# A list scheduler with another model of the engines, and one matmul of a gated unit on 128 rows instead of 64

## The chip, the core and the metric

The program runs on one core of one Trainium2 chip. TensorE (PE) multiplies matrices into PSUM, VectorE (DVE) and ScalarE (ACT) work on tiles, GpSimd (POOL) works on tiles and issues a few DMAs, SyncE (SP) issues the other DMAs. Every engine takes its instructions in the order in which the program lists them for it, and waits where an instruction needs something that isn't ready. The metric is the device time of one execution in microseconds, lower is better.

## The reference

```python
g = sigmoid((u * gate_w).sum(-1))                       # one gate per token
# a: state space convolution, 448 channels, 256 modes each, 2048 tokens
dt = exp(log_dt); A = -exp(log_A_real) + 1j * A_imag; C = (C_real + 1j * C_imag) * dt
K = 2 * einsum("dn,dnl->dl", C, exp(A * dt * pos)).real
a = irfft(rfft(u, 4096) * rfft(K, 4096))[:2048] + u * D_skip
# b: gated linear unit, 448 -> 1792 -> 448
b = (sigmoid(x @ w_gate) * (x @ w_up)) @ w_down
out = g * a + (1 - g) * b
```

All is float32; the outputs have 2048 tokens of 448 channels.

## The kernel before

The kernel has three bodies of work that it runs side by side. An instruction isn't issued where it stands in the source: the source records it by `op` (line 156), with its engine, an estimated duration, what it reads and writes and a priority. `Plan.order` (line 185) then builds the order of all engines by a list schedule: it keeps a clock for each engine, takes the engine that can start something earliest, and on it the ready instruction with the least priority number. `Plan.emit` (line 270) issues them in that order.

**The gated unit** has 14 tiles of 128 hidden units, two halves of 1024 tokens (H), and two blocks of 512 tokens in each (B). Values are split into a high and a low part, each of which TensorE takes in one pass (type float32r); a product is high × high + high × low + low × high. `glu_w` (line 957) loads the weights of a tile, ScalarE rounds them to the high part (`wh`, `vh`, L969), and GpSimd, or VectorE for the last tiles, makes the low part (`wl`, `vl`, L971). `glu_mm` (line 990) multiplies a block of 512 tokens by the weights of 128 hidden units in eleven matmuls. The 448 channels make three blocks of 128 (L995 high × high, L996 high × low, L997 low × high) and one of 64. The last block of the tokens, `x[:, 3]`, holds the high part on the rows 0 to 63 and the low part on the rows 64 to 127, and the weights of these channels stand on both halves of the rows, so L999 does two products at once, and L1000, the eleventh, does low × high. A gate and an up product make one unit (`glu_up`): tanh on ScalarE (L983), the product on VectorE (L984), the split of the result (L986, L987). `glu_down` (line 1005) multiplies back to 448 channels (L1012 to L1014), and VectorE adds the result to `ob` (L1028). There are 112 runs of `glu_mm` and 224 triples of the way down.

**The convolution's kernels.** `params` (line 581) makes the phases and powers of the modes at the start, mostly on VectorE with W = 1024 columns, some on ScalarE and GpSimd. `kgen` (line 895) makes 16 channels at a time, 28 chunks in two halves, each chunk in two half-chunks: phases on TensorE (`tp`, L827, L842), sine and cosine on ScalarE, powers on GpSimd (`tb`, L803 to L816), products of powers and phases on VectorE (L866 to L885), and 32 small matmuls with 32 weight columns each (`kp`, L890). A half's kernels go to DRAM (`kd`).

**The transforms.** A class `Chain` (line 371) takes 224 channels through a two-stage Fourier transform: a first stage with weights on 64 rows (`stage1_pair`, L442, or `stage1_split`, L432 and L433), a transpose (by a detour through DRAM, `shf`, or on VectorE, L453, for the last half), and a second stage with 64 weight columns (`spectrum_pair`, L471). The tokens go first (`spectrum_u`), then each half of the kernels: product with the tokens' spectrum (`product_pair`, L500 to L511) and the way back (`back`, L546, L550). The half 0 works in `fx_fu`, `uax` and `ubx`, the half 1 in `fx_fk`, `ua` and `ub`.

What sets the order is the estimates. TensorE's are c_mm = 0.4167 ns per column and 3 ns, whatever the shape; the 16 small matmuls of a half-chunk are 680 ns; VectorE and GpSimd don't disturb each other; a DMA takes 640 ns to issue and then its bytes at 350 per ns on one wire, with no limit to how many are under way. A change of TensorE's shape, which is the number of rows and of weight columns that a matmul uses (128 × 128, 64 × 128, 128 × 64, 128 × 32), costs nothing in this model. The priorities of the parts are at line 300: parameters 10, kernel generation 20, tokens' transform 30, kernels' transform 40 and 41, gated unit 60, which fills in.

Of the kernel before, what the change touches and what calls it, by code (L numbers as in the profile page):

```python
# [25 lines left out]
SPC, KPC, ACC = 640.0, 680.0, 93.0  # L26
# [12 lines left out]
LN2 = math.log(2.0)  # L39
# [4 lines left out]
# channel order of the kernel generation: (half, chunk, column tile, q)  # L44
# [8 lines left out]
def shape_tables():  # L53
    """Transform matrices and position grids: functions of the shapes alone."""
# [22 lines left out]
        # rows (c g k2) to rows (g c l2), the inverse  # L77
# [17 lines left out]
# functions that one table set of ScalarE holds  # L95
# [3 lines left out]
class Res:  # L99
    """Something that instructions read and write: a virtual tile or a DRAM tensor."""  # L100

    def __init__(self, pool=None, tag=None, shape=None, dt=None, name=None, real=None):
        self.pool, self.tag, self.shape, self.dt, self.name = pool, tag, shape, dt, name
        self.real = real
        self.log = []
        self.users = 0
        self.done = 0.0
        self.live = real is not None
# [8 lines left out]
class Pool:  # L117
    def __init__(self, plan, name, space, after, below):
        self.plan, self.name, self.space, self.after, self.below = plan, name, space, after, below
        self.stack, self.tp = ExitStack(), None  # L120
        self.left, self.end, self.tags = 0, 0.0, {}

    def tile(self, tag, bufs, shape, dt=F32):
        q = self.tags.setdefault(tag, dict(free=[0.0] * bufs, n=0, next=0, bufs=bufs))
# [18 lines left out]

class Plan:
# [11 lines left out]
    def op(self, eng, cost, fn, r=(), w=(), prio=0, after=(), size=0, table=None):  # L156
        me = dict(i=len(self.ops), eng=eng, cost=cost, fn=fn, prio=prio, size=size, table=table,
                  deps=set(), outs=[], res=[], new=[], ready=0.0, order=[a["i"] for a in after])
# [14 lines left out]
        for res in me["res"]:  # L173
            if res.pool is not None:
                res.users += 1
                res.pool.left += 1
# [8 lines left out]
    def order(self):  # L185
        ops = self.ops
        need = []
        for o in ops:
            o["deps"].discard(o["i"])
            o["deps"] |= set(o["order"])  # L190
            for d in o["deps"]:
                ops[d]["outs"].append(o["i"])
            need.append(len(o["deps"]))
        engines = sorted({o["eng"] for o in ops})
        free = {e: 0.0 for e in engines}
        cand = {e: [] for e in engines}
        for o in ops:
            if need[o["i"]] == 0:
                cand[o["eng"]].append(o)
        wire, table, seq, left = 0.0, (), [], len(ops)  # L200

        def start_of(o):
            t = o["ready"]
            for x in o["new"]:
                p = x.pool
                for a in p.after:
                    if a.left:
                        return None
                    t = max(t, a.end)
                q = p.tags[x.tag]  # L210
                if q["next"] != x.idx or not q["free"]:
                    return None
                t = max(t, min(q["free"]))
            return t

        while left:
            best = None
            for e in engines:
# [8 lines left out]
                te = max(lo, free[e])  # L227
# [12 lines left out]
            fin = te + cost  # L240
            if o["size"]:
                wire = max(wire, fin) + o["size"] / 350.0
                fin = wire + 1500.0
            for x in o["new"]:
                q = x.pool.tags[x.tag]
# [894 lines left out]
```

## Time and profile before

| what | value |
|---|---|
| median of 3 runs | 884.44 us (884.14 to 885.29) |
| span of the profiled execution | 878.0 us |
| median less span | 6.4 us |
| mean granted clock of TensorE | 0.972 |
| ScalarE, GpSimd busy | 501.3, 330.1 us |
| DMA | 115.66 MB, 132 GB/s on average |

The profile gives the span from the first instruction to the last of one execution; no other time of that execution is given. A line "L995 PE MATMUL gu_gps<-xs_glu,wh_glu" is the matmul at line 995 that writes the PSUM tile gu of the pool gps from the tiles xs and wh. A matmul's row in the timeline begins at its start; its duration reaches to the modelled end of its last column, while the next one has already started.

### The profile page before, as it was taken

The page shows a single profiled execution, that of the slowest core. Times are in us where ns is not written, and L with a number is a line of the kernel's source. Part 1 is how long each engine was busy: PE and PEld are TensorE (multiplying, and loading weights), DVE is VectorE, ACT ScalarE, POOL GpSimd, SP SyncE. Part 2 cuts the span into 40 slices and gives each one's busy share as a digit, 9 for nine tenths or more (in the row PEclk, how much of TensorE's full clock was granted, in tenths as well). Part 3 has the DMA queues.
Part 4 walks back from the last instruction along what each step waited for, and adds up shares of the span by engine and source line. Part 5 has one row for each costly group of instructions (what it writes and reads, how often), then busy time and mean ns, then how long its engine had stood idle before and what let it go on. Part 6 is the DMA issues. An engine that isn't in the chain of part 4 may idle for free. (4 is left out here: it accounts for less than half of the span.)

```text
span 878.0 us, 16776 instructions
## 1 busy us (share of the span) xinstructions
PE 808.5 (92%) x6688; PEld 541.5 (62%) x6688; DVE 733.0 (83%) x982; ACT 501.3 (57%) x862; POOL 330.1 (38%) x358
## 2 busy tenths in 40 slices
PE   4988799999988999999998999999989999889987
PEld 2665576666655667776665666666766566445543
DVE  2869984798995999999897989899846788978995
ACT  3544654677766877777677987777722352221210
POOL 3367644454452645374355535645021120000000
PEclk9989999899997999999999999999999999998999
DMA  9951377222290326436494116422959953294324
GB/s 242 226 107 32 97 216 168 95 95 93 81 194 26 125 83 146 160 116 157 135 219 120 44 60 180 125 84 79 208 104 248 280 153 109 70 212 119 85 56 117
DMA packets 95831, 115.66 MB, mean 132 GB/s; under 512 B 31465, under 2 KB 80937, under 8 KB 95241
## 3 DMA queue, kind: packets, MB, share of 16 engines
q1 hardware_dynamic: 93704, 110.98, 48.4%
q0 software_dynamic: 2048, 3.61, 1.6%
q8 instruction: 53, 0.87, 0.4%
q14 instruction: 26, 0.20, 0.1%
HBM read 78.32 MB, written 36.24 MB: 130 GB/s over the span
## 5 line engine op out<-in xcount | busy, mean ns | idle before, releaser
L995 PE MATMUL gu_gps<-xs_glu,wh_glu 128*128 128x512 f32 x336 | 148.0, 440 | 11.7 <-ACT wh_glu L969 11.6
L866 DVE TENSOR_TENSOR es_eg<-tb_eg 128x512 f32<-128x512 f32 x168 | 125.5, 772 | 20.7 <-PE kp_egp L890 19.2
L997 PE MATMUL gu_gps<-xs_glu,wl_glu 128*128 128x512 f32 x336 | 135.3, 403 | 1.2 <-POOL wl_glu L971 1.2
L996 PE MATMUL gu_gps<-xs_glu,wh_glu 128*128 128x512 f32 x336 | 135.5, 403 | 0.0
L1012 PE MATMUL dn_gps<-vh_glu,hh_glu 128*128 128x448 f32 x224 | 98.6, 440 | 7.0 <-ACT ob_glu L1021 3.5
L971 POOL TENSOR_TENSOR wl_glu<-xr_glu,wh_glu 128x512 fp32r<-128x512 f32 x44 | 77.8, 1777 | 65.7 <-ACT wh_glu L969 65.7
L995 PEld LDWEIGHTS gu_gps<-xs_glu,wh_glu 128*128 128x128 f32 x336 | 65.6, 195 | 41.2 <-issue 19.0
L1013 PE MATMUL dn_gps<-vh_glu,hl_glu 128*128 128x448 f32 x224 | 83.7, 374 | 4.5 <-DVE hl_glu L987 4.5
L1014 PE MATMUL dn_gps<-vl_glu,hh_glu 128*128 128x448 f32 x224 | 83.6, 373 | 0.5 <-POOL vl_glu L971 0.5
L884 DVE TENSOR_TENSOR ec_eg<-ec_eg,es_eg 128x1024 f32<-128x1024 f32 x56 | 79.8, 1426 | 0.0
L997 PEld LDWEIGHTS gu_gps<-xs_glu,wl_glu 128*128 128x128 f32 x336 | 65.3, 194 | 18.0 <-POOL wl_glu L971 2.8
L813 POOL TENSOR_TENSOR tb_eg<-tb_eg 128x96 f32<-128x96 f32 (+2 forms) x84 | 73.4, 877 | 5.8
L827 PE MATMUL tp_egp<-pos_sb,ph_eg 96*128 96x512 f32 x168 | 72.5, 446 | 1.9 <-ACT fr_eg L845 1.7
L885 DVE TENSOR_TENSOR es_eg<-fr_eg,es_eg 128x1024 f32<-128x1024 f32 x56 | 73.3, 1310 | 0.3
L996 PEld LDWEIGHTS gu_gps<-xs_glu,wh_glu 128*128 128x128 f32 x336 | 65.8, 196 | 10.0 <-issue 1.3
L971 POOL TENSOR_TENSOR vl_glu<-vr_glu,vh_glu 128x448 fp32r<-128x448 f32 x24 | 35.5, 1477 | 87.0 <-ACT vh_glu L969 85.5
L1012 PEld LDWEIGHTS dn_gps<-vh_glu,hh_glu 128*128 128x128 f32 x224 | 42.9, 191 | 39.0 <-issue 17.1
L803 POOL MEMSET tb_eg<- 128x96 f32 x28 | 7.8, 283 | 152.0 <-DVE es_eg L866 152.0
L1028 DVE SCALAR_TENSOR_TENSOR ob_glu<-dn_gps,og,ob_glu 128x448 f32<-128x448 f32 x72 | 49.1, 681 | 18.4 <-PE dn_gps L1014 17.7
L859 ACT ACTIVATE ec_eg<-ec_eg,half_pi 128x1024 f32<-128x1024 f32 x56 | 63.9, 1140 | 0.0
L471 PE MATMUL fps_fups<-fx_fu,m_sb 128*64 128x224 f32 x384 | 48.7, 376 | 15.6 <-DMA fx_fu<-shf 7.8
L984 DVE SCALAR_TENSOR_TENSOR sg_glu<-sg_glu,gu_gps 128x512 f32<-128x512 f32 x56 | 38.1, 682 | 24.8 <-PE gu_gps L1000 18.1
(167 smaller groups left out, 1720.0 us busy)
## 6 DMA issues: line engine op xcount, KB each, us to landing
shf<-fx_fu SPq DMA_DIRECT2D x16, 896.0 KB
fx_fu<-shf SPq DMA_DIRECT2D x16, 896.0 KB
xr_glu<-in_w_dram SPq DMA_DIRECT2D x52, 256.0 KB
us<-fx_fu SPq DMA_DIRECT2D x4, 1792.0 KB
vr_glu<-in_w_dram SPq DMA_DIRECT2D x28, 224.0 KB
gt_pro<-in_u_dram SPq DMA_DIRECT2D x8, 448.0 KB
fx_fu<-in_u_dram SPq DMA_DIRECT2D x8, 448.0 KB
kd<-ke_eg SPq DMA_DIRECT2D x8, 448.0 KB
```

The lines of the kernel that those rows point to most:

```text
L813: pool(96 * m, lambda n=n, m=m: G.tensor_mul(g3(n + 1, m), g3(1, m), g3(n, 1).to_broadcast([128, 32, 3, m])))
L827: T.matmul(tp.real, ph[:, c % 2, 128 * nh:128 * nh + 128].bitcast(F32R), pos[:, 512 * i:512 * i + 512], start=True, stop=last)
L866: V.tensor_mul(o.rearrange("p d (i k) -> p d i k", k=ny), x.unsqueeze(3).to_broadcast([128, 16, nx, ny]), y.unsqueeze(2).to_broadcast([128 ...
L884: op("DVE", c_dve(1024), lambda: V.tensor_mul(ec[:, :, 0:64], ec[:, :, 0:64], es[:, :, 0:64]), [es], [ec], prio)
L885: op("DVE", c_dve(1024), lambda: V.tensor_mul(es[:, :, 0:64], fr.real, es[:, :, 0:64]), [fr], [es], prio)
L971: op(eng, cost(n), lambda: e.tensor_sub(view(l), a(), view(h).bitcast(F32)), [res, (h, key)], [(l, key)], prio)
L995: T.matmul(p.real, wh[:, k, cs], x[:, k], start=(k == 0), stop=False)
L996: T.matmul(p.real, wh[:, k, cs], x[:, 4 + k], start=False, stop=False)
L997: T.matmul(p.real, wl[:, k, cs], x[:, k], start=False, stop=False)
L1012: T.matmul(p[:, :D], hh[:, ts], vh.real, start=(i == 0), stop=False)
L1013: T.matmul(p[:, :D], hl[:, ts], vh.real, start=False, stop=False)
L1014: T.matmul(p[:, :D], hh[:, ts], vl.real, start=False, stop=(i == len(fs) - 1))
```

## The change

Eight things change in the scheduler, all in the estimates and in the rule:

- TensorE: 0.4167 ns per column and 13 ns, float32 matmuls as four passes; a change of shape costs 92, 104 or 196 ns by its neighbours; after a window of 3.4 us with over 1.4 us idle the next one runs at half rate.
- VectorE and GpSimd: instructions with two operands in SBUF hold one port, one engine at a time; fixed times and the times of half-height tiles are set apart.
- SP: 400 ns to issue, at most eight DMAs under way, a rate for each kind of DMA.
- ScalarE: other fixed times for operands in PSUM and for scale or bias by column.
- Delays between engines are 33 to 78 ns and a tail for each engine instead of 200 to 260.
- Buffers of a tile are taken in turn.
- Ten priorities are set apart by a table `RANK`, whose key is engine, tile and old priority.
- The scheduler's state is kept out of the recorded instructions, and most comments are gone.

In the computation one line changes: L1000 multiplies all 128 rows, so that the low part of the weights also meets the low part of the last 64 channels. That adds a product of two low parts, and it writes the same PSUM tile.

```diff
+RANK = {
+    ('Act', 'hh', 45): 41.5,
...
+class Clock:
+    ISSUE, CAST, FLIGHT = 400.0, 600.0, 8
+    WINDOW, IDLE = 3413.0, 1400.0
+    TAIL = dict(PE=175.0, DVE=78.0, Pool=40.0, Act=110.0)
...
+            for hold, port, lead in o["cost"]:
+                t += lead
+                if port:
+                    t = self.port = max(t, self.port) + hold
...
+    def matmul(self, mode, cost, t):
+        if self.mode not in (None, mode):
+            cost += 196.0 if self.fresh else 92.0
+            self.fresh = True
+        elif self.fresh:
+            cost += 104.0
+            self.fresh = False
...
-    HOP, HPE = 200.0, 260.0
+    HOP, HPE, HPOOL = 33.0, 60.0, 78.0
...
-            cost = o["cost"]
-            if o["table"] is not None and o["table"] not in table:
-                table = next(x for x in TABLES if o["table"] in x)
-                cost += 1300.0
-            free[e] = te + cost
...
+            fin = clock.run(o, te)
...
-def c_mm(n, passes=1):
-    return (max(0.4167 * n, 106.0) + 3.0) * passes
+def c_mm(n, count=1, mode=FULL):
+    return [(mode, 0.4167 * n + 13.0)] * count
+def c_mm4(n, count=1, mode=FULL):
+    return [(mode, (1.6667 * n + 4.0) * count * mode[1] / 128)]
...
                 T.matmul(p.real, wh[:, 3, cs], x[:, 3], start=False, stop=False)
-                T.matmul(p.real, wl[0:64, 3, cs], x[0:64, 3], start=False, stop=True)
+                T.matmul(p.real, wl[:, 3, cs], x[:, 3], start=False, stop=True)
```

Every engine's queue is in another order. The counts of the instructions are the same on every engine. Lines of the changed kernel stand 90 further down in these parts: L1000 is L1090 there, L827 is L917, L1012 is L1102, L866 is L956, L318 (every DMA of SP) is L408.

TensorE, where the kernel generation begins (gu: products up, dn: products down, tp: phases). Before:

```order
L999 MATMUL gu_gps_961<-xs_glu_107,wh_glu_869 128x512
L1000 MATMUL gu_gps_961<-xs_glu_107,wl_glu_879 128x512
L1012 MATMUL dn_gps_1004<-vh_glu_628,hh_glu_881 128x448
L1013 MATMUL dn_gps_1004<-vh_glu_628,hl_glu_897 128x448
L1014 MATMUL dn_gps_1004<-vl_glu_633,hh_glu_881 128x448
L995 MATMUL gu_gps_991<-xs_glu_107,wh_glu_869 128x512
L996 MATMUL gu_gps_991<-xs_glu_107,wh_glu_869 128x512
L997 MATMUL gu_gps_991<-xs_glu_107,wl_glu_879 128x512
L827 MATMUL tp_egp_1048<-pos_sb,ph_eg_1002 128x512
L827 MATMUL tp_egp_1052<-pos_sb,ph_eg_1002 128x512
```

After:

```order
L1102 MATMUL dn_gps_1315<-vh_glu_1061,hh_glu_1214 128x448
L1103 MATMUL dn_gps_1315<-vh_glu_1061,hl_glu_1219 128x448
L1104 MATMUL dn_gps_1315<-vl_glu_1068,hh_glu_1214 128x448
L1085 MATMUL gu_gps_1300<-xs_glu_116,wh_glu_1110 128x512
L1086 MATMUL gu_gps_1300<-xs_glu_116,wh_glu_1110 128x512
L1087 MATMUL gu_gps_1300<-xs_glu_116,wl_glu_1119 128x512
L532 MATMUL fps_fups_1340<-fx_fu_1286,ft_fu_1289 128x224 x2
L917 MATMUL tp_egp_1350<-pos_sb,ph_eg_1268 128x512
L917 MATMUL tp_egp_1356<-pos_sb,ph_eg_1268 128x512
L1089 MATMUL gu_gps_1300<-xs_glu_116,wh_glu_1110 128x512
L1090 MATMUL gu_gps_1300<-xs_glu_116,wl_glu_1119 128x512
```

Ahead of the first tp stand 281 products up and 120 down before, and 383 and 192 after, and a first pair of the tokens' transform (L532, on 64 rows) has come ahead of it too.

VectorE at the same place (ob: sums of the gated unit, th and bsx: parameters, es and tb: first chunk). Before:

```order
L593 SCALAR_TENSOR_TENSOR th_pro_917<-th_pro_917,tg_pro_912 128x896
L1028 SCALAR_TENSOR_TENSOR ob_glu_524<-dn_gps_930,og,ob_glu_524 128x448
L747 TENSOR_TENSOR bsx_pro_965<-th_pro_917,ex_pro_899 128x2x14x32
L984 SCALAR_TENSOR_TENSOR sg_glu_958<-sg_glu_958,gu_gps_954 128x512
L1028 SCALAR_TENSOR_TENSOR ob_glu_557<-dn_gps_970,og,ob_glu_557 128x448
```

After:

```order
L1118 SCALAR_TENSOR_TENSOR ob_glu_540<-dn_gps_1247,og,ob_glu_540 128x448
L1074 SCALAR_TENSOR_TENSOR sg_glu_1240<-sg_glu_1240,gu_gps_1235 128x512
L1118 SCALAR_TENSOR_TENSOR ob_glu_558<-dn_gps_1282,og,ob_glu_558 128x448
L1077 TENSOR_TENSOR hl_glu_1337<-sg_glu_1240,hh_glu_1330 128x512
L1118 SCALAR_TENSOR_TENSOR ob_glu_579<-dn_gps_1315,og,ob_glu_579 128x448
L956 TENSOR_TENSOR es_eg_1365<-tb_eg_1298 128x16x32 x3
```

The parameters' last steps stood among the last sums before; after, gated-unit steps alone stand there: 17 L984, 17 L987 and 16 L1028 come ahead of the first chunk instead of 13, 13 and 8.

SP where the last half's kernels have gone to DRAM (kd) and come back as fx (uax, ua: the tokens' spectrum for the two halves; ftx, ft: tables). Before:

```order
L318 DMA kd_61<-ke_eg_4273 2048x1x56 x4
L318 DMA xr_glu_6906<-in_w_dram 128x512
L318 DMA vr_glu_6915<-in_w_dram 128x448
L318 DMA xr_glu_6923<-in_w_dram 128x512
L318 DMA xr_glu_6944<-in_w_dram 128x512
L318 DMA xr_glu_6952<-in_w_dram 128x512
L318 DMA uax_fk_6983<-us_58 128x448
L318 DMA uax_fk_6991<-us_58 128x448
L318 DMA uax_fk_7000<-us_58 128x448
L318 DMA ftx_fk_7008<-in_t1t_dram 128x512
L318 DMA fx_fk_7017<-kd_61 64x1792 x7
```

After, from the third uax on (ahead of it kd, one xr and two uax):

```order
L408 DMA uax_fk_7041<-us_58 128x448
L408 DMA ftx_fk_7047<-in_t1t_dram 128x512
L408 DMA ua_fk_7054<-us_59 128x448
L408 DMA ua_fk_7060<-us_59 128x448
L408 DMA ua_fk_7066<-us_59 128x448
L408 DMA ft_fk_7068<-in_t1t_dram 128x512
L408 DMA ft_fk_7078<-in_t1t_dram 128x512
L408 DMA fx_fk_7080<-kd_61 64x1792
L408 DMA uax_fk_7092<-us_58 128x448
L408 DMA uax_fk_7115<-us_58 128x448
L408 DMA uax_fk_7136<-us_58 128x448
L408 DMA fx_fk_7080<-kd_61 64x1792 x5
```

The weights' loads have moved ahead of kd, the loads of ua and ft ahead of fx, and three loads of uax now split the eight loads of fx.

More of the change, by code (lines that the diff above doesn't have):

```diff
@@ L38 @@
 FIRST = ('Act', 'Act')
-LN2 = math.log(2.0)
+HALF, SHORT = 240.0, 208.0
 MAGIC = 12582912.0
@@ L120, in __init__ @@
         self.stack, self.tp = ExitStack(), None
-        self.left, self.end, self.tags = 0, 0.0, {}
+        self.tags = {}
     def tile(self, tag, bufs, shape, dt=F32):
-        q = self.tags.setdefault(tag, dict(free=[0.0] * bufs, n=0, next=0, bufs=bufs))
+        q = self.tags.setdefault(tag, dict(n=0, bufs=bufs))
         r = Res(self, tag, list(shape), dt, f"{tag}_{self.name}{q['n']}")
@@ L141, in real, with __init__, when, run @@
         return self.real_pool().tile(r.shape, r.dt, tag=r.tag, name=r.name, bufs=self.tags[r.tag]["bufs"])
+class Clock:
+    ISSUE, CAST, FLIGHT = 400.0, 600.0, 8
+    WINDOW, IDLE = 3413.0, 1400.0
+    TAIL = dict(PE=175.0, DVE=78.0, Pool=40.0, Act=110.0)
+    def __init__(self, engines):
+        self.free = {e: 0.0 for e in engines}
+        self.port = self.wire = self.last = 0.0
+        self.flight, self.mode, self.fresh, self.table, self.idle = [], None, False, (), {}
+    def when(self, e, t):
+        t = max(t, self.free[e])
+        return max(t, self.flight[0]) if e == "SP" and len(self.flight) >= self.FLIGHT else t
+    def run(self, o, t):
+        e = o["eng"]
+        if o["size"]:
+            self.free[e] = t + (self.ISSUE if e == "SP" else self.CAST)
+            self.wire = max(self.wire, self.free[e] + 1000.0) + o["cost"]
+            end = self.wire + 550.0
+            if e == "SP":
+                self.flight = self.flight[1 if len(self.flight) >= self.FLIGHT else 0:]
+                self.flight.append(max([end] + self.flight[-1:]))
+            return end
+        if e == "Act":
+            if o["table"] is not None and o["table"] not in self.table:
+                self.table = next(x for x in TABLES if o["table"] in x)
+                t += 1300.0
+            t += o["cost"]
+        elif e == "PE":
+            for mode, cost in o["cost"]:
+                t = self.matmul(mode, cost, t)
+        else:
+            for hold, port, lead in o["cost"]:
+                t += lead
+                if port:
+                    t = self.port = max(t, self.port) + hold
+                else:
+                    t += hold
+        self.free[e] = t
+        return t + self.TAIL[e]
+    def matmul(self, mode, cost, t):
[5 more added lines that the diff above has]
+            self.fresh = False
+        self.mode = mode
+        W, a = self.WINDOW, self.last
+        while a < t:
+            k = int(a // W)
+            b = min(t, (k + 1) * W)
+            self.idle[k] = self.idle.get(k, 0.0) + b - a
+            a = b
+        while cost > 1e-3:
+            k = int(t // W)
+            rate = 0.5 if self.idle.get(k - 1, 0.0) > self.IDLE else 1.0
+            step = min(cost / rate, (k + 1) * W - t + 1e-3)
+            t, cost = t + step, cost - step * rate
+        self.last = t
+        return t
@@ L156, in op @@
     def op(self, eng, cost, fn, r=(), w=(), prio=0, after=(), size=0, table=None):
-        me = dict(i=len(self.ops), eng=eng, cost=cost, fn=fn, prio=prio, size=size, table=table,
-                  deps=set(), outs=[], res=[], new=[], ready=0.0, order=[a["i"] for a in after])
+        x = w[0][0] if isinstance(w[0], tuple) else w[0]
+        key = eng, x.tag or x.name, prio
+        me = dict(i=len(self.ops), eng=eng, cost=cost, fn=fn, key=key, prio=RANK.get(key, prio), size=size, table=table,
+                  deps=set(), res=[], new=[], order=[a["i"] for a in after])
         for kind, lst in (("r", r), ("w", w)):
@@ L226, in order @@
                     continue
-                te = max(lo, free[e])
+                te = clock.when(e, lo)
                 if best is None or te < best[0]:
@@ L264, in order @@
             seq.append((te, len(seq), o))
-            left -= 1
-        self.length = max(free.values())
+        self.length = max(clock.free.values())
         seq.sort(key=lambda x: (x[0], x[1]))
@@ L508, in product_pair @@
             for i in range(2):
[L509 removed]
+                op("DVE", 2 * c_dve(HD, half=True), lambda i=i: add(i), [ub], [(x, r)], prio)
             z = self.psum(1)
[L511 removed]
+            op("PE", c_mm4(D), lambda: T.matmul(z[:, :D], m_sb[:, 128:256], self.pair(r), start=True, stop=True),
                [(x, r), m_sb], [z], prio)
```

221 lines of the change are left out of this document (115 added, 106 removed).

## The prediction

> **What bounds the kernel now.** I read the page first (busy shares and slices), then the stretches of the run, the waits, and last the timeline of TensorE around one product.
>
> ```profile
> span 878.0 us, 16776 instructions
> PE 808.5 (92%) x6688; PEld 541.5 (62%) x6688; DVE 733.0 (83%) x982; ACT 501.3 (57%) x862; POOL 330.1 (38%) x358
> PE   4988799999988999999998999999989999889987
> DVE  2869984798995999999897989899846788978995
> ```
>
> TensorE is busy for 92% of the span and VectorE for 83%. The two rows of slices show both near nine tenths for most of the run, so no single number tells which one binds. I cut the span where the kernel generation begins and ends on VectorE:
>
> ```profile
> L866 DVE TENSOR_TENSOR es_eg<-tb_eg x168: 675/684/1784, 148.6 to 628.2; 128x512 f32<-128x512 f32 x168
> L885 DVE TENSOR_TENSOR es_eg<-fr_eg,es_eg x56: 1206/1216/2312, 162.2 to 640.3; 128x1024 f32<-128x1024 f32 x56
> core 0: us, PE busy (x) PEld busy (x) DVE busy (x) ACT busy (x) POOL busy (x), PEclk, DMA share, GB/s
> 0.00:148.60 148.60, 122.48 (x449) 87.12 (x449) 107.89 (x143) 71.82 (x115) 79.64 (x58) 0.93 0.65 153
> 148.60:640.30 491.70, 470.53 (x5206) 323.38 (x5205) 443.42 (x552) 371.58 (x641) 234.73 (x280) 0.98 0.44 120
> 640.30:739.00 98.70, 95.39 (x466) 61.70 (x465) 65.85 (x113) 35.09 (x68) 15.70 (x21) 0.98 0.73 190
> 739.00:757.00 18.00, 14.35 (x67) 8.61 (x65) 17.78 (x12) 2.79 (x6) 0.00 (x0) 1.00 0.15 46
> 757.00:829.00 72.00, 65.54 (x312) 38.37 (x313) 60.67 (x116) 16.21 (x29) 0.00 (x0) 0.95 0.60 145
> 829.00:845.00 16.00, 13.17 (x51) 7.86 (x52) 15.86 (x9) 1.31 (x3) 0.00 (x0) 1.00 0.00 0
> 845.00:878.00 33.00, 27.02 (x146) 14.46 (x145) 21.57 (x43) 2.49 (x4) 0.00 (x0) 0.99 0.46 115
> ```
>
> The head (to 148.6) holds gated-unit work and the mode parameters. The middle (148.6 to 640.3) is the kernel generation: PE is busy 470.5 of 491.7, 96%, VectorE 443.4, 90%. The tail is 237.7 us long: PE 215.5 busy by the five rows, VectorE 181.7. What VectorE waits for is mostly TensorE that is late (us in all, times, longest):
>
> ```profile
> DVE es_eg L866 <- PE kp_egp L890: 19.2, 19, 3.0
> DVE sg_glu L984 <- PE gu_gps L1000: 18.1, 9, 3.6
> DVE ob_glu L1028 <- PE dn_gps L1014: 17.7, 16, 4.4
> DVE ec_eg L881 <- ACT ec_eg L859: 14.9, 12, 8.3
> ```
>
> **The widened product.** Matmuls overlap, so the price of one is the distance from its start to the next start:
>
> ```profile
> L1000 PE MATMUL gu_gps<-xs_glu,wl_glu 64*128 64x512 f32 x112 | 56.9, 508 | 0.0
> 300.33 0.39 PE L997 MATMUL gu_gps<-xs_glu,wl_glu 128*128 128x512 f32 x1
> 300.56 0.36 PE L1012 MATMUL dn_gps<-vh_glu,hh_glu 128*128 128x448 f32 x1
> 300.76 0.37 PE L1013 MATMUL dn_gps<-vh_glu,hl_glu 128*128 128x448 f32 x1
> 300.97 0.36 PE L1014 MATMUL dn_gps<-vl_glu,hh_glu 128*128 128x448 f32 x1
> 301.17 0.40 PE L999 MATMUL gu_gps<-xs_glu,wh_glu 128*128 128x512 f32 x1
> 301.50 0.49 PE L1000 MATMUL gu_gps<-xs_glu,wl_glu 64*128 64x512 f32 x1
> 301.92 0.47 PE L1012 MATMUL dn_gps<-vh_glu,hh_glu 128*128 128x448 f32 x1
> 302.23 0.36 PE L1013 MATMUL dn_gps<-vh_glu,hl_glu 128*128 128x448 f32 x1
> ```
>
> Between neighbours of the full shape, 512 columns take 0.23 us (300.33 to 300.56) and 448 take 0.20. Around the 64-row L1000 it is otherwise: L999 takes 0.33, L1000 0.42, and the L1012 behind it 0.31. That is 0.10 + 0.19 + 0.11 = 0.40 us for one trip into another shape and back, 0.20 per change of shape. The first row counts 112 L1000. In the order of TensorE, shape changes (full, 64 rows, 64 columns, 32 columns) fall from 702 to 474: 228 × 0.20 = 45.6 us of TensorE's time. Runs of 64 rows fall from 188 to 80, so nearly all of it is L1000; the new order by itself removes about a dozen changes.
>
> The Trainium skill, "TensorEngine Tiling (Array Packing)", Key Properties, says that a change of tiling mode drains TensorE; the 0.40 agrees. The same page, When to Use Tiling, advises row tiling for a contraction of 64 or fewer, which speaks for the narrow form; by that rule two narrow products could share one 0.23 and widening would lose 112 × 0.23 / 2 = 13 us. The 0.42 behind L1000 shows no such sharing here.
>
> **What moves, stage by stage.** Counted in the two orders of TensorE (gated-unit products up, then down, then changes of shape): head 281, 120, 50 before and 383, 192, 1 now; middle 688, 363, 442 and 613, 294, 319; tail 263, 189, 210 and 236, 186, 154. By 0.23, 0.20 and 0.20 us, TensorE's work changes by +23.5 + 14.4 − 9.8 = +28.1 in the head, −17.3 − 13.8 − 24.6 = −55.7 in the middle, −6.2 − 0.6 − 11.2 = −18.0 in the tail. The sum is −45.6 again.
>
> Head. These rows show where it starts and ends on TensorE:
>
> ```profile
> 11.59 0.79 PE L995 MATMUL gu_gps<-xs_glu,wh_glu 128*128 128x512 f32 x1 [11.59 <-ACT wh_glu L969]
> 141.03 0.63 PE L827 MATMUL tp_egp<-pos_sb,ph_eg 96*128 96x512 f32 x2
> ```
>
> The work before the first kernel-generation product is 281 × 0.23 + 120 × 0.20 + 50 × 0.20 = 98.6 us. With the 11.6 before the first matmul that is 110.2, and the product came at 141.0: 30.8 us went to waits and to the clock of 0.93. Now the work is 126.7, so the product can come at 138.3 if TensorE never waits, and at 169.1 if it loses the same 30.8. It stands behind all that work in TensorE's queue, and VectorE's first chunk behind it.
>
> ```profile
> L987 DVE TENSOR_TENSOR hl_glu<-sg_glu,hh_glu 128x512 fp32r<-128x512 f32 x56 | 47.7, 858 | 6.7 <-ACT hh_glu L986 6.5
> L984 DVE SCALAR_TENSOR_TENSOR sg_glu<-sg_glu,gu_gps 128x512 f32<-128x512 f32 x56 | 38.1, 682 | 24.8 <-PE gu_gps L1000 18.1 <-ACT wh_glu L969 6.4
> L1028 DVE SCALAR_TENSOR_TENSOR ob_glu<-dn_gps,og,ob_glu 128x448 f32<-128x448 f32 x72 | 49.1, 681 | 18.4 <-PE dn_gps L1014 17.7
> la_pro<-in_lat_dram SPq DMA_DIRECT2D x1, 448.0 KB
> 22.00:44.00 22.00, 19.85 (x71) 13.41 (x72) 19.02 (x45) 13.25 (x25) 7.65 (x6) 0.92 1.02 224
> ```
>
> VectorE's queue has 4 L984, 4 L987 and 8 L1028 more ahead of the chunk; its 40.7 idle us of the head cover them, and without that cover they cost 4 × 0.68 + 4 × 0.86 + 8 × 0.68 = 11.6. The load of la, now the first on SP's queue, is 448 KB ahead of the first tokens: 2 us at the 224 GB/s of a stretch full of loads. The bounds of the head are −3 and +28; I take the middle, **+12**.
>
> Middle. TensorE needs 470.5 − 55.7 = 414.8 and no longer binds; VectorE is late next. It has 4 L984, 3 L987 and 8 L1028 less: 10.7 us, so 432.7 of work, and it had 48.3 us of waits. Lost in full, these waits give 432.7; kept in full, 481.0. Three of the four largest rows of waits name TensorE, the fourth ScalarE, which does not get faster, so I take half, 24.2: 456.9, which is **−35** against 491.7.
>
> The port that VectorE and GpSimd share is the unknown of this stage:
>
> ```profile
> L866 DVE TENSOR_TENSOR es_eg<-tb_eg 128x512 f32<-128x512 f32 x168 | 125.5, 772 | 20.7 <-PE kp_egp L890 19.2
> L884 DVE TENSOR_TENSOR ec_eg<-ec_eg,es_eg 128x1024 f32<-128x1024 f32 x56 | 79.8, 1426 | 0.0
> L884 DVE TENSOR_TENSOR ec_eg<-ec_eg,es_eg x56: 1210/1224/2322, 160.3 to 638.5; 128x1024 f32<-128x1024 f32 x56
> ```
>
> L866, with both operands in SBUF, has a median of 684 ns and a mean of 772, L884 1224 and 1426, while L984, which reads PSUM, stays at 682. The excess is 168 × 0.088 + 56 × 0.202 = 26 us. An order that keeps GpSimd's work beside VectorE's reads of PSUM could win up to 26; GpSimd's 234.7 us packed into 457 instead of 491.7 would make the excess 8% larger, +2. The counts of both engines' work are unchanged, so I take 0.
>
> Tail. The last half's kernels pass a chain: store, load, first stage, transposes (739 to 757), product, transposes (829 to 845), way back. The new order lets this half pass the other on VectorE, and puts TensorE's gated-unit products beside the transposes. Against it, on SP's queue three loads of uax, each of which waits for VectorE to free a buffer, now stand ahead of five of the eight loads of fx:
>
> ```profile
> 646.41 8.93 SPq L318 DMA_DIRECT2D kd<-ke_eg  x4
> 664.16 8.88 SPq L318 DMA_DIRECT2D fx_fk<-kd  x7
> ```
>
> The floor is VectorE's 181.7 plus the 23.9 us until the first of those loads (640.3 to 664.2): 205.6, −32. The ceiling is 0, if the chain alone sets the tail. I take **−16**, near TensorE's −18.
>
> Sum: 878.0 + 12 − 35 − 16 = 839. The median of the runs is 884.4, 6.4 more than the span; what lies around the span I take as unchanged: **845 us**.
>
> **The rivals.**
> - *The waits go too.* The head costs nothing, the middle loses all its waits (−59), the tail −16: 803 + 6.4 = 809. For it: 45.6 us of TensorE's work is gone. Against it: with TensorE at 96%, VectorE still had 48 us of waits, and some name ScalarE.
> - *TensorE's gain turns into idle time.* VectorE keeps its 48.3: head +12, middle −10.7, tail −6 (a third of the −18): 873 + 6.4 = 880. For it: VectorE at 90%, and ScalarE's row of waits.
> - *The queue holds the kernel generation back (slower).* TensorE's queue has 174 more gated-unit products ahead of the first kernel-generation product. With the old loss of 30.8 this comes 28 us late, the middle wins only its 10.7, the tail nothing: 895 + 6.4 = 902. It decides against the change from where the delay passes 10.7 plus what the tail wins.
> - *The shape is not what costs.* If the wide L1000 kept its 0.42 and its neighbours theirs, the head would gain 37.9 us of work and no relief: 98.6 + 37.9 + 11.6 + half of 30.8 puts the first product at 163.5, +22; the middle wins 10.7, the tail its 6.8 of moved products: +5, 889. The rows of L997, full shape and the same columns, speak against it.
>
> The Trainium skill, "SBUF — State Buffer", Who interferes with whom, calls the port that VectorE and GpSimd share an exclusive lock, which agrees with the longest L866 of 1784 against 684 ns; by it the second rival becomes likelier when the middle is packed, since no order then hides GpSimd's work under VectorE's two-input instructions.
>
> **How the numbers follow.** Chances: forecast 0.55, waits go too 0.16, idle time 0.14, held back 0.12, shape 0.03. With one term at its end and the others as taken, the forecast lies between 821 (middle −59) and 869 (middle −11). The range reaches over most of the ground of the first two rivals, 811 to 885; left out are the two slow cases, 0.15, and about a third of the first rival, 0.05. About 0.2% is what a measurement can tell from no change, and some 0.04 of the second rival, 4 us from the time before, falls within it: faster 0.55 + 0.16 + 0.10 = 0.81, within 0.04, slower 0.12 + 0.03 = 0.15.
>
> **What would show it.** L1000 with the rows 128*128 and a start-to-start of 0.23; the first L827 (line 917 of the changed kernel) between 138 and 169; VectorE busy over 92% of the middle; the middle's PE share well under 96%; waits of VectorE for PE cut to half; the five-row tail near 222. Wrong would be a middle still near 490 with VectorE waiting for ScalarE or GpSimd, or a head beyond 175.

## The result and the profile after

The changed kernel takes 852.98 us (median of 4 runs, 849.87 to 853.36), the kernel before 884.87 us on the same chip. The ratio is 0.9637 with a 95% interval of 0.961 to 0.9664. The prediction was 845 us, in a range of 811 to 885. The profiled execution took 853.36 us with a span of 851.6. Executions of one kernel differ by up to 2.7%, the longer ones mostly at a lower granted clock, and while the medians count all of them, the ratios leave out those over 1.5% above the kernel's fastest.

The page of the changed kernel, first its span, then busy time and share, then the busy tenths of TensorE and VectorE in 40 slices:

```profile
span 851.6 us, 16799 instructions
PE 777.9 (91%) x6688; PEld 548.4 (64%) x6688; DVE 738.9 (87%) x982; ACT 503.9 (59%) x862; POOL 329.3 (39%) x358
PE   4699999899999986999869999999999699999977
DVE  2798997489999999999979998999986689989975
```

TensorE's busy time fell by 30.6 us (808.5 to 777.9), the span by 26.4. VectorE's rose by 5.9. The stretches of the changed kernel, cut at the same instructions as before (first es, last es, and the two sets of transposes of the tail), except that 819 lies 4.7 us behind the end of the last transpose:

```profile
core 0: us, PE busy (x) PEld busy (x) DVE busy (x) ACT busy (x) POOL busy (x), PEclk, DMA share, GB/s
0.00:158.90 158.90, 135.49 (x591) 112.02 (x591) 120.91 (x158) 78.09 (x123) 83.27 (x66) 0.97 0.62 154
158.90:631.10 472.20, 444.04 (x5099) 311.07 (x5099) 438.92 (x537) 370.24 (x636) 232.88 (x275) 0.96 0.45 122
631.10:719.00 87.90, 78.55 (x413) 50.19 (x412) 65.81 (x117) 32.78 (x64) 13.14 (x19) 0.96 0.84 217
719.00:733.80 14.80, 14.15 (x63) 11.23 (x63) 14.77 (x6) 2.90 (x5) 0.00 (x0) 1.00 0.04 13
733.80:799.00 65.20, 63.93 (x326) 38.55 (x327) 60.43 (x116) 15.16 (x28) 0.00 (x0) 1.00 0.65 160
799.00:819.00 20.00, 15.90 (x62) 12.50 (x61) 16.29 (x8) 3.42 (x6) 0.00 (x0) 0.88 0.00 1
819.00:851.60 32.60, 25.81 (x141) 12.85 (x139) 21.78 (x44) 1.26 (x2) 0.00 (x0) 0.97 0.47 116
```

The head grew by 10.3 us (148.6 to 158.9). The middle shrank by 19.5 (491.7 to 472.2), the tail by 17.2 (237.7 to 220.5), of which 10.8 went in its first stretch, up to the transposes (98.7 to 87.9), and 6.8 in the stretch between the two sets of transposes (72.0 to 65.2).

What VectorE waited for in the middle of the changed kernel (us in all, times, longest):

```profile
DVE es_eg L956 <- POOL tb_eg L906: 7.6, 4, 4.7
DVE ec_eg L971 <- ACT ec_eg L949: 7.3, 15, 1.0
DVE fr_eg L923 <- ACT fr_eg L922: 6.7, 2, 5.9
DVE es_eg L956 <- PE kp_egp L980: 5.9, 8, 1.3
DVE ob_glu L1118 <- PE dn_gps L1104: 0.8, 1, 0.8
DVE sg_glu L1074 <- PE gu_gps L1090: 0.5, 1, 0.5
```

The same view of before, in its own middle:

```profile
DVE es_eg L866 <- PE kp_egp L890: 19.2, 19, 3.0
DVE ec_eg L881 <- ACT ec_eg L859: 14.9, 12, 8.3
DVE fr_eg L833 <- ACT fr_eg L832: 5.2, 7, 1.5
DVE sg_glu L984 <- PE gu_gps L1000: 4.7, 4, 3.6
DVE ob_glu L1028 <- PE dn_gps L1014: 2.8, 3, 1.8
DVE es_eg L866 <- POOL tb_eg L816: 0.7, 1, 0.7
```

The waits for PE fell from 26.7 to 7.2 us, and the largest wait for ScalarE (ec) from 14.9 to 7.3. The wait for the powers from GpSimd (tb) grew from 0.7 to 7.6, that for ScalarE's fr from 5.2 to 6.7.

The widened product, in the timeline of TensorE (start, duration, line):

```profile
289.80 0.39 PE L1087 MATMUL gu_gps<-xs_glu,wl_glu 128*128 128x512 f32 x1
290.03 0.39 PE L1089 MATMUL gu_gps<-xs_glu,wh_glu 128*128 128x512 f32 x1
290.26 0.39 PE L1090 MATMUL gu_gps<-xs_glu,wl_glu 128*128 128x512 f32 x1
290.48 0.39 PE L1085 MATMUL gu_gps<-xs_glu,wh_glu 128*128 128x512 f32 x1
```

L1090 now has all rows, and from start to start it takes 0.22 us instead of 0.42, as its neighbours do (0.23).

### The profile page after: what moved, and what is told of

It is laid out like the page before. It is cut to its first block, busy times and chain, and to the rows that moved or that the text cites. A ratio compares the mean times of both kernels' runs of the same rounds, so it can differ in the third digit from the quotient of the medians.

```text
span 851.6 us, 16799 instructions
## 1 busy us (share of the span) xinstructions
PE 777.9 (91%) x6688; PEld 548.4 (64%) x6688; DVE 738.9 (87%) x982; ACT 503.9 (59%) x862; POOL 329.3 (39%) x358
## 5 line engine op out<-in xcount | busy, mean ns | idle before, releaser
L1085 PE MATMUL gu_gps<-xs_glu,wh_glu 128*128 128x512 f32 x336 | 141.3, 420 | 18.7 <-ACT wh_glu L1059 11.2
L1086 PE MATMUL gu_gps<-xs_glu,wh_glu 128*128 128x512 f32 x336 | 133.8, 398 | 0.0
L956 DVE TENSOR_TENSOR es_eg<-tb_eg 128x512 f32<-128x512 f32 x168 | 119.4, 762 | 14.6 <-POOL tb_eg L906 7.6
L1102 PE MATMUL dn_gps<-vh_glu,hh_glu 128*128 128x448 f32 x224 | 94.9, 424 | 7.2 <-ACT hh_glu L1076 5.0
L1085 PEld LDWEIGHTS gu_gps<-xs_glu,wh_glu 128*128 128x128 f32 x336 | 64.5, 192 | 42.9 <-ACT wh_glu L1059 11.2
L1061 POOL TENSOR_TENSOR wl_glu<-xr_glu,wh_glu 128x512 fp32r<-128x512 f32 x44 | 79.0, 1806 | 28.6 <-ACT wh_glu L1059 28.6
L917 PE MATMUL tp_egp<-pos_sb,ph_eg 96*128 96x512 f32 x168 | 75.7, 476 | 14.7 <-ACT fr_eg L935 7.5
L903 POOL TENSOR_TENSOR tb_eg<-tb_eg 128x96 f32<-128x96 f32 (+2 forms) x84 | 78.9, 943 | 6.1
L974 DVE TENSOR_TENSOR ec_eg<-ec_eg,es_eg 128x1024 f32<-128x1024 f32 x56 | 80.6, 1438 | 0.0
L975 DVE TENSOR_TENSOR es_eg<-fr_eg,es_eg 128x1024 f32<-128x1024 f32 x56 | 77.8, 1390 | 1.9
L1061 POOL TENSOR_TENSOR vl_glu<-vr_glu,vh_glu 128x448 fp32r<-128x448 f32 x24 | 38.0, 1582 | 104.6 <-ACT vh_glu L1059 91.6
L1086 PEld LDWEIGHTS gu_gps<-xs_glu,wh_glu 128*128 128x128 f32 x336 | 64.7, 192 | 11.3 <-issue 0.9
L893 POOL MEMSET tb_eg<- 128x96 f32 x28 | 7.8, 284 | 156.4 <-DVE es_eg L956 152.2
L459 ACT ACTIVATE fx_fu<-fps_fups 128x448 f32<-128x448 f32 x80 | 44.1, 551 | 39.2 <-PE fps_fups L561 19.9
L1102 PEld LDWEIGHTS dn_gps<-vh_glu,hh_glu 128*128 128x128 f32 x224 | 43.3, 193 | 35.2 <-issue 13.4
L949 ACT ACTIVATE ec_eg<-ec_eg,half_pi 128x1024 f32<-128x1024 f32 x56 | 63.9, 1141 | 0.0
```

The source lines that it names most:

```text
L903: pool(96 * m, lambda n=n, m=m: G.tensor_mul(g3(n + 1, m), g3(1, m), g3(n, 1).to_broadcast([128, 32, 3, m])))
L917: T.matmul(tp.real, ph[:, c % 2, 128 * nh:128 * nh + 128].bitcast(F32R), pos[:, 512 * i:512 * i + 512], start=True, stop=last)
L956: V.tensor_mul(o.rearrange("p d (i k) -> p d i k", k=ny), x.unsqueeze(3).to_broadcast([128, 16, nx, ny]), y.unsqueeze(2).to_broadcast([128 ...
L974: op("DVE", c_dve(1024), lambda: V.tensor_mul(ec[:, :, 0:64], ec[:, :, 0:64], es[:, :, 0:64]), [es], [ec], prio)
L975: op("DVE", c_dve(1024), lambda: V.tensor_mul(es[:, :, 0:64], fr.real, es[:, :, 0:64]), [fr], [es], prio)
L1061: op(eng, cost(n), lambda: e.tensor_sub(view(l), a(), view(h).bitcast(F32)), [res, (h, key)], [(l, key)], prio)
```

## The experiments

Each run is named with its time, and with its ratio to the kernel before on the same chip. "Gated" counts the gated unit's matmuls, up and down together. The stages are cut as above, in the one profiled execution of each run, whose span is given. A median is a time, which is 1.8 us more than a span; where the two are further apart than that, the stages are those of an execution that is longer or shorter than the usual one. The last two columns are explained below.

| run | median us | profiled span | head | middle | tail | gated in the middle | gated left | us left |
|---|---|---|---|---|---|---|---|---|
| before | 882 to 885 | 878.0 | 148.6 | 491.7 | 237.7 | 1013 | 58 | 33.3 |
| after | 852.98 | 851.6 | 158.9 | 472.2 | 220.5 | 899 | 56 | 37.3 |
| e1 wide, old order | 870.03 | 870.0 | 144.3 | 486.3 | 239.4 | 1010 | 58 | 32.9 |
| e2 narrow, new order | 864.06 | 859.4 | 166.0 | 473.7 | 219.7 | 895 | 56 | 35.1 |
| e3 less VectorE | 839.87 | 844.3 | 159.1 | 467.0 | 218.2 | 897 | 56 | 36.4 |
| e4 less TensorE | 851.24 | 857.3 | 161.4 | 475.2 | 220.7 | 734 | 47 | 34.3 |
| ea less ScalarE | 848.01 | 841.9 | 157.6 | 467.9 | 216.4 | 899 | 56 | 36.3 |
| ep less port | 840.40 | 836.2 | 153.3 | 463.7 | 219.2 | 891 | 56 | 36.3 |
| e5 no table | 885.73 | 888.4 | 160.7 | 467.9 | 259.8 | 801 | 210 | 77.4 |
| e7 no port in the model | 889.45 | 894.9 | 142.2 | 501.6 | 251.1 | 988 | 139 | 58.7 |
| rh four of the table | 859.25 | 858.8 | 158.1 | 469.5 | 231.2 | 890 | 90 | 49.1 |
| rt six of the table | 886.70 | 877.7 | 156.7 | 463.4 | 257.6 | 811 | 192 | 73.8 |
| er table, old model | 885.78 | 892.3 | 147.7 | 510.8 | 233.8 | 1030 | 72 | 40.1 |
| pm23 phases on PE | 865.07 | 877.1 | 156.4 | 463.4 | 257.3 | 857 | 139 | 58.7 |

### The two parts apart

e1 is the kernel before with the wide product alone:

```diff
-                T.matmul(p.real, wl[0:64, 3, cs], x[0:64, 3], start=False, stop=True)
+                T.matmul(p.real, wl[:, 3, cs], x[:, 3], start=False, stop=True)
```

> The kernel before with L1000 on all 128 rows and nothing else; the order of every engine stays word for word. Shape changes of TensorE fall from 702 to about 485. Theory A (TensorE gets the 0.40 us per product back, but the middle is then bound by VectorE): TensorE's work falls by about 44 us, of which the middle can use only what VectorE waited for TensorE (27 us there), the head and the tail some 10 between them: 852 to 865 us. Rival B (TensorE binds everywhere): 840. Rival C (the shape is not what costs): 884 and a start-to-start of 0.42 behind L1000 as before.

e2 is the changed kernel with the narrow product, the same edit backwards.

> The changed kernel with L1090 back on 64 rows; the order of every engine is that of the changed kernel. Theory A: TensorE's work rises by about 44 us, the middle, which VectorE binds at 93%, hides 10 to 20 of it: 873 to 890 us, so that the new order alone is worth 0 to 10 us. Rival B (TensorE binds everywhere): 897. Rival C (the order is what counts): 853 to 857.

Measured: e1 870.03 us (867.24 to 871.78), ratio 0.9854 (0.982 to 0.9887); e2 864.06 (861.12 to 866.5), ratio 0.9787 (0.975 to 0.9824). Before was 882.14 there. So the wide product alone is worth 12.1 us and the order alone 18.1, together 30.2; the change gave 31.9 beside its own runs of before. The parts add up, and the order is the larger, though the intervals of the two ratios just touch. Neither time lies in a range that was expected: e1 falls between those of theory A and rival C, e2 between rival C and theory A. This is the stretch of the middle of e1:

```profile
144.30:630.60 486.30, 454.59 (x5195) 327.99 (x5194) 445.54 (x550) 369.30 (x639) 237.01 (x280) 0.97 0.44 121
```

And that of e2:

```profile
166.00:639.70 473.70, 452.14 (x5095) 304.87 (x5096) 440.68 (x537) 371.70 (x636) 229.29 (x275) 0.97 0.44 122
```

TensorE is busy about equally long in both, 16 and 18 us less than in before. Yet the middle of e1 is 5.4 us shorter than before's, that of e2 18.0. What TensorE does in the middle is therefore not what the middle's length follows. On the new order the wide product shortens the head most (166.0 to 158.9), the middle by 1.5 and the tail not at all (219.7 and 220.5).

### One engine's work taken away

All four start from the changed kernel and keep its order.

e3:

```diff
-V.tensor_mul(es[:, :, 0:64], fr.real, es[:, :, 0:64])
+V.tensor_mul(es[:, 0:8, 0:64], fr[:, 0:8], es[:, 0:8, 0:64])
```

> The changed kernel in its own order, with L975 (the product of sines and powers) over 8 of 16 channels, so half of that product is left out: VectorE's work falls by 56 times about 0.7 us, 37 to 40 us, all of it in the middle. Theory A (VectorE binds the middle at 93%): the middle, 474 us, falls by 20 to 35, until TensorE with its 446 us binds; 820 to 835 us. Rival B (TensorE binds the middle): under 8 us, 845 to 853.

e4 (the line L1086, in the loop over the three full blocks of channels):

```diff
-                T.matmul(p.real, wh[:, k, cs], x[:, 4 + k], start=False, stop=False)
```

> The changed kernel in its own order without L1086 (high part of the weights times low part of the tokens is left out): TensorE does 336 matmuls of 0.23 us less, 77 us: about 24 in the head, 39 in the middle, 15 in the tail. Theory A (VectorE binds the middle): the middle falls by less than 10 us, head and tail by 5 to 15 each: 820 to 840 us. Rival B (TensorE binds everywhere): 776 to 785 us.

ea (L949):

```diff
-            ec[:, :, 0:64], ec[:, :, 0:64], AF.Sin, scale=-TWO_PI, bias=half_pi.real)
+            ec[:, 0:8, 0:64], ec[:, 0:8, 0:64], AF.Sin, scale=-TWO_PI, bias=half_pi.real)
```

> The changed kernel in its own order, with L949 (a sine) on 8 of 16 channels, so half of that sine is left out: ScalarE's work in the middle falls by 56 times about 0.55 us, 31 us of 370. Theory A (neither engine alone binds the middle, each half-chunk passes through all four in turn): the middle falls by 5 to 15 us, as with VectorE's 37 us less, which gave 13: 838 to 848 us. Rival B (ScalarE binds): the middle falls by 25 or more, 822 to 830 us. Rival C (ScalarE has room): under 3 us, 850 to 854 us.

ep (L1061, where GpSimd makes the low parts):

```diff
-e.tensor_sub(view(l), a(), view(h).bitcast(F32))
+e.tensor_sub(view(l), a(), view(h).bitcast(F32)) if eng == "DVE" else e.memset(view(l).bitcast(F32), 0.0)
```

> The changed kernel in its own order, with GpSimd's low parts of the gated unit's weights (L1061 on GpSimd) set to zero by a memset instead of a subtraction, so low times high is left out for these tiles: GpSimd reads no SBUF in some 120 us of its 330. Theory A (GpSimd's reads stretch VectorE's instructions: L956 762 against 687 ns, L974 1438 against 1225, L975 1390 against 1226): the means fall by a third to a half of the excess, VectorE's work in the middle by 8 to 15 us, the middle by 5 to 12, 840 to 848 us in all. Rival B (the port does not stretch VectorE): means as they were, 851 to 854 us.

Measured, beside the 852.98 us and the ratio of 0.9637 (0.961 to 0.9664) of the changed kernel: e3 839.87 us, ratio 0.9522 (0.9471 to 0.9573), 13 us less, or 10 by the ratios; e4 851.24, ratio 0.9619 (0.9563 to 0.9676), no difference; ea 848.01, ratio 0.9579 (0.9524 to 0.9634), 5 us less, with an interval that overlaps the change's; ep 840.40, ratio 0.9516 (0.9464 to 0.9567), 13 us less, or 11 by the ratios. No range that was expected holds for e3, which lies between theory A and rival B, or for e4, which lies above theory A; ea and ep lie at the two ends of their theory A.

In e4 three of the eleven matmuls of every run of `glu_mm` are gone. The stretches of e4: the whole middle, then the products up (gu) alone (there the columns are PE busy, clock, DMA share, GB/s):

```profile
161.40:636.60 475.20, 426.96 (x4937) 285.20 (x4939) 438.38 (x537) 369.96 (x636) 231.57 (x275) 0.93 0.44 121
161.40:636.60 475.20, 126.81 (x440) 0.93 0.44 121
```

The products up alone in the middle of the changed kernel:

```profile
158.90:631.10 472.20, 162.10 (x605) 0.96 0.45 122
```

165 products fewer are 165 × 0.23 = 38 us of TensorE at the full rate, and the middle is no shorter. Head and tail are no shorter either (161.4 and 220.7). The profiled execution is the longest of e4's four (859.04 us, the others 844.83 to 853.99), so a few us of gain may be missing in these stages, but not the 77 us that were left out. TensorE's granted clock fell as well (see the last section), so part of the relief never became free time. Even so, TensorE's amount of work sets none of the three stages of the changed kernel, though its row of slices is at nine tenths nearly throughout.

VectorE's work in e3 was cut by about 30 us in the middle (438.9 to 408.5); its profiled execution, the longest of that run's, has a middle 5.2 us shorter, and the median is 13 lower. What is left of the saving turned into waits: of the middle, VectorE was idle 33.3 us in the changed kernel and 58.5 in e3. The cut was smaller than the 37 us expected, and 10 to 13 of its 30 us were won over the run, a third to four tenths. In ea ScalarE's busy time in the middle fell by 20.6 us (370.2 to 349.6), which won 5, not clear of noise. So none of the three engines that were cut alone binds the middle, and VectorE is the only one of them whose microseconds clearly count. GpSimd wasn't cut alone. That the middle is a ring of PE, ScalarE, GpSimd and VectorE that hand half-chunks on is a reading of the waits, not shown by a run.

ep bears on what GpSimd costs VectorE. The multiplication at L975 in the groups of instructions of the middle (busy us, mean ns), in before, where it is L885:

```profile
L885 DVE TENSOR_TENSOR es_eg<-fr_eg,es_eg 128x1024 f32<-128x1024 f32 x56 | 73.3, 1310 | 0.3
```

In the changed kernel:

```profile
L975 DVE TENSOR_TENSOR es_eg<-fr_eg,es_eg 128x1024 f32<-128x1024 f32 x56 | 77.8, 1390 | 1.9
```

In ep:

```profile
L975 DVE TENSOR_TENSOR es_eg<-fr_eg,es_eg 128x1024 f32<-128x1024 f32 x56 | 70.7, 1262 | 1.9
```

With low parts that GpSimd writes without reading, the mean falls from 1390 to 1262 ns, and VectorE's busy time in the middle from 438.9 to 417.4 us, with the same instructions. The Trainium skill, "SBUF — State Buffer", Who interferes with whom, says that a VectorE instruction with two SBUF inputs contends with a GpSimd instruction that reads SBUF and not with one that only writes; the 21.5 us agree. The run doesn't tell reading from being busy, though: the memsets are also shorter than the subtractions, and GpSimd's busy time in the middle fell from 232.9 to 181.0 us. Nor is all of the 11 to 13 us won shown to be the port's, since VectorE's wait for the powers (L906) fell too, from 7.6 to 2.4 us.

### The model and its table

e5 is the changed kernel with an empty table, e7 the changed kernel whose model gives VectorE and GpSimd no shared port:

```diff
-RANK = { ... }
+RANK = {}
```

> The changed kernel with an empty table of priorities, so that the new engine model alone makes the order (head 399 products up and 192 down, middle 534 and 270, tail 299 and 210). Theory A (the table lets the last half pass the other in the tail, and the tail's 17 us came from there): the tail back at 230 to 240 us, 862 to 872 us in all. Rival B (the engine model made the tail shorter): a tail of 218 to 224 us and 850 to 858 us.

```diff
-                if port:
+                if False:
```

> The changed kernel planned without the shared port (VectorE and GpSimd never hold each other up in the plan). Its order starts the kernel generation after 278 products up and 120 down, as the kernel before did, instead of 383 and 192. Theory A (the middle is a chain of coupled queues, and a plan that knows the port makes it shorter): the head falls to 140 to 148 us, the middle rises by 15 or more to 487 to 500, 856 to 870 us in all. Rival B (the port in the plan is worth nothing): head 140 to 148, middle 468 to 480, tail as it is, 838 to 850 us.

Measured: e5 885.73 us (874.89 to 890.21), ratio 1.0012 (0.9973 to 1.005); e7 889.45 (881.93 to 900.91), ratio 1.0046 (1.0003 to 1.0089). Every number that was expected of e5 was too low: the new model without the ten priorities, and with the wide product, is no faster than the kernel before. The loss is in the tail (259.8 us against 220.5), not in the head or the middle. e7 was above all that was expected of it as well. Its head of 142.2 is as expected, and its middle of 501.6 just past the 500 of theory A; that the tail would grow to 251.1 was in neither theory.

So the table was cut in two, and put on the old model (er: the kernel before with the wide product, the table and its key):

```diff
-                  ... prio=prio, size=size, table=table,
+        key = eng, x.tag or x.name, prio
+                  ... prio=RANK.get(key, prio), size=size, table=table,
```

> The order's gain is tied to the table of ten priorities: without it the new model gave 885.7 us with the wide matmul, as long as the kernel before. This run takes the table alone: before's engine model and costs, the wide matmul, and the ten priorities. Theory A (the table alone carries the gain; the model is of little weight): 850 to 858 us. Theory B (the table was fitted to the new model's order and means nothing without it): 865 us or more, near or above the 870.0 of the old order with the wide matmul.

rh keeps acr, th0, ci and la, rt the other six:

> The changed kernel with four of its ten priorities, those of the stage before the kernel generation (acr, th0, ci, la). The trace without any of the ten has its loss in the tail: 259.9 us from the last L975 on, beside 220.5, with a head of 160.7 beside 158.9. Theory A (the six others, on ob, ub, ubx, fps, fx and hh, set the tail): 875 to 890 us with a tail over 245. Theory B (the list is chaotic, and any of the ten moves everything): a tail between 220 and 240.

> The changed kernel with the six other priorities (ob, ub, ubx, fps, fx, hh). Theory A (those six set the tail): 850 to 862 us, tail 215 to 228, head near 160. Theory B (any of the ten moves everything): a tail of 235 or more and over 868 us.

Measured: er 885.78 us, ratio 1.0006 (0.9962 to 1.005); rh 859.25, ratio 0.9732 (0.9669 to 0.9795); rt 886.70, ratio 1.0027 (0.9988 to 1.0066). On the old model the table costs 15.8 us (885.78 against the 870.03 of e1). That is theory B of er. For rh and rt theory A failed both times and the numbers of theory B held, the other way round from what the names suggest: the six priorities of the tail's own work alone win nothing (886.70 against 885.73), while four priorities of the head take 26.5 us off, nearly all of it in the tail (259.8 to 231.2) and little in the head (160.7 to 158.1). The six are worth another 6 to 8 on top of the four (6.3 by the times, 0.0095 by the ratios).

Head and middle come out much alike in the four orders that the whole model makes, with ten, four, six or no priorities (head 157 to 161 us, middle 463 to 472). With the port taken out of the model the middle is 502 us, and on the old model it is 486 without the table and 511 with it. By these orders the model makes the middle short, and under it the table decides the tail.

What the tail answers to shows in its end. These rows are the stretch behind the last transpose of the changed kernel: all engines, then TensorE's products up and the products down alone:

```profile
814.30:851.60 37.30, 29.30 (x148) 15.66 (x148) 22.93 (x47) 1.89 (x3) 0.00 (x0) 0.91 0.41 102
814.30:851.60 37.30, 4.95 (x11) 0.91 0.41 102
814.30:851.60 37.30, 13.05 (x45) 0.91 0.41 102
```

The same three rows of e5:

```profile
811.00:888.40 77.40, 65.97 (x302) 44.71 (x302) 38.12 (x68) 7.82 (x13) 0.00 (x0) 0.90 0.21 52
811.00:888.40 77.40, 28.36 (x99) 0.90 0.21 52
811.00:888.40 77.40, 30.21 (x111) 0.90 0.21 52
```

In the changed kernel 56 gated matmuls are left over when the last transpose ends, in e5 210, and e5 needs 40 us more from there. The last two columns of the table hold this for all fourteen traces. A straight line through them, 20.3 us + 0.277 us for each matmul left, meets every one within 4 us. No run takes the matmuls left at the end away alone, so this is a relation between traces; that TensorE is busy for 66.0 of the 77.4 us there in e5 speaks for its being the cause. So gated matmuls that run beside the kernel generation or the transforms cost next to nothing, as e4 says too, and those that are left when nothing else remains cost about their full time. e5 has 98 fewer in the middle than the changed kernel (801 and 899), and its middle is only 4.3 us shorter: 0.04 us for each there, against 0.28 behind the last transpose.

Why four priorities of the parameters lead to about 90 more gated matmuls in the middle isn't shown; which of the four does it wasn't tried. Nor were the other parts of the model (the price of a shape change, eight loads under way, the clock) tried alone.

### A version that might be faster

pm23 moves phases from VectorE to TensorE and ScalarE:

```diff
-PEM = (1, 2)
+PEM = (2, 3)
```

> Phases of two of every three half-chunks on TensorE and ScalarE, instead of every second: nine more half-chunks, so 18 of L923 (0.68 us each) less on VectorE, about 12 us; on ScalarE about 1.5 us more for each of nine, 13 us; on TensorE 36 matmuls more. By the slopes of the relief runs (13 us for 37 us of VectorE's work, 5 for 31 of ScalarE's, none for TensorE's) 12 x 0.36 - 13 x 0.16 = 2 us less: 848 to 854. A rival has that the list made for other counts loses the tail: the order of the tail changes, and the time is over 862.

Measured: 865.07 us (862.36 to 881.29), ratio 0.9777 (0.9682 to 0.9871); the rival held. The middle did become shorter, 463.4 against 472.2 us. But the new costs made another list, which left 139 gated matmuls behind the last transpose instead of 56: by the line (139 − 56) × 0.277 = 23 us, more than was won. The profiled execution is 13.8 us longer than the median (878.87 us), so not all of its tail of 257.3 us is typical. Of the kernels that compute all of the reference, none beat the changed one.

## Why the prediction was right, and where not

The forecast, faster with time won in the middle and the tail and some lost in the head, held. The time was 8 us above the 845. The direction of each stage was right, but the reason given, TensorE's lighter work, accounts for 12 of the 32 us (e1). The order is worth 18 (e2), and that the head and the tail came out within 2 us of the forecast is in part luck, as the steps show:

- **The price of the trip.** 0.40 us around a 64-row product, 0.20 per change, was right: L1090 goes at 0.22 from start to start, and the rival that the shape isn't what costs is refuted. Widening alone won 12.1 us, where two narrow products that share one slot would have made it lose 13. But most of what this saves TensorE did not become time. By the prediction 45.6 us of TensorE's time go; e1, whose TensorE is busy 33.4 us less than before (808.5 to 775.1), gives 12.1 us, and e4, with three of eleven products out of every unit, nothing more.
- **Head, +12, measured +10.3.** The size was right, the mechanism was not. The first phase product came at 160.8, inside the 138 to 169, but TensorE's queue was not what the head waited for. VectorE's first chunk doesn't stand behind that product: it began at 158.9, 1.9 us ahead of it. These are VectorE's first instruction of the kernel generation, and before it GpSimd's powers, in the timeline of the changed kernel:

```profile
153.19 0.63 POOL L896 TENSOR_SCALAR tb_eg<-bs_eg 128x96 f32<-128x96 f32 x2 [3.21 <-DMA bs_eg<-bsd]
157.76 1.36 POOL L906 TENSOR_TENSOR tb_eg<-tb_eg,bs_eg 128x32 f32<-128x32 f32 x6
158.93 4.68 DVE L956 TENSOR_TENSOR es_eg<-tb_eg 128x512 f32<-128x512 f32 x6 [1.63 <-POOL tb_eg L906]
```

  VectorE waits for GpSimd's powers, these for the load of a table of the parameters. e4 took 24 us of products off the head (278 products up instead of 383, at 0.23), and its kernel generation began at 161.4, no earlier. ep, which spares GpSimd and VectorE work in the head (83.3 to 48.1 and 120.9 to 101.3 us busy), began at 153.3. With the narrow product the queue does count: in e2 TensorE is busy 12.3 us longer in the head, and the generation began at 166.0.
- **Middle, −35, measured −19.5.** This term was mis-sized, by 15.5 us in two parts. VectorE's work was to fall by 10.7 to 432.7, and its busy time fell by 4.5 to 438.9: as many instructions went as counted (552 to 537), and the durations of all, counts times means, fell by 10 us as forecast (481 to 471); the busy time fell by less since the rows of neighbours overlap by 32 us instead of 38. The term for the port was taken as 0 within −26 and +2. By the means of L866, L884 and L885 it came out near +3.5: 168 × (762 − 772) + 56 × (1438 − 1426) + 56 × (1390 − 1310) ns. ep shows that what GpSimd does to make the low parts still costs VectorE 21.5 us in the new order. And half of the 48.3 us of waits was to go, 24.2 to stay; 33.3 stayed. The rows behind that half were those of the whole execution; in the middle alone they name TensorE for 26.7 us and ScalarE for 20.1. The waits for PE did fall to about a quarter, and ScalarE's for ec to half although ScalarE got no faster, but those for GpSimd's powers and for ScalarE's fr rose. That VectorE, late next, was busy over 92% of the middle held, just (438.9 of 472.2, 93%); TensorE's share fell only from 96 to 94%, its busy time to 444.0 us instead of the 414.8 of the sum. Some 5 us of this come from two cuts that don't match: the products were counted from the first phase product on, at 141.0 us, and the middle starts at 148.6, with 25 gated matmuls between the two. The rest isn't taken apart.
- **Tail, −16, measured −17.2.** The size was right. The reason given, TensorE's −18, fits the sum (its busy time there fell from 215.5 to 198.3) but not the runs apart: with the wide product alone the tail is 239.4, with the order alone 219.7. All of the tail's gain is the order's, which the prediction named beside it without a price, so that the size came out is luck, and e4 shows that with yet less TensorE work nothing more is to be had.
- **What lies around the span, 6.4, was 1.8.** 853.36 less 851.6 is 1.76, and 871.78 less 870.0 in e1 is 1.78. By that the profiled execution of before took about 879.8 us, 4.6 less than the median of the runs: the 6.4 mixed the two. The sum of 839 for the span missed 851.6 by 12.6, and the 4.6 hid a part of that. It also means that a stage of before is uncertain by a few us in these comparisons.
- **The rivals.** "The queue holds the kernel generation back" didn't happen, since the queue wasn't what the generation waited for. "TensorE's gain turns into idle time" is the truest of them as a mechanism (e4 shows it alone), but at 880 it left the order's own gain out. No rival said that the list's gain hangs on ten priorities: without them the change would have come out within measurement of no change.

## What to carry to other kernels

Where filler work runs beside a chain, count what is left of it when the chain ends: in these traces it cost about its full time there, and next to nothing earlier, so read the last stretch of the span before the busy shares. A busy share of 94% proved no bound here; taking a part of one engine's work away, in an unchanged order, told in one run which engine's microseconds count. A list schedule that was fitted with hand-set priorities to one set of costs must be fitted again when a cost, a priority or the work changes, since any of these can lose more than the model wins.

## What was not expected of the hardware

With less work TensorE was granted a lower clock: 0.93 in the middle of e4 and 0.96 in the changed kernel, while its share of busy time was 89.8 and 94.0% (before 95.7% at 0.98, e5 92.6% at 0.94). All four executions of e4 show it, with 0.93 to 0.95 over the whole run against 0.96 to 0.97. e1 and e7 are against a simple rule, 0.97 at 93.5 and at 92.6%. So the 38 us of products that e4 leaves out took only 17.1 us off the busy time of its middle (444.0 to 427.0). Whether the idle time lowered the clock, or both come from something else, wasn't tested.
